# A fused RWKV-5 and dense kernel with a written order: loads from two queues, products in the order of their sums, an arctangent for small h, state products and levels in one run

## The chip, the cores and the metric

The kernel runs on one core of one Trainium2 chip. The metric is the device time of one execution in microseconds. TensorE is called PE here, VectorE DVE, ScalarE ACT, GpSimd POOL and SyncE SP, as in the profile.

## The reference

Two blocks follow each other. The first is a linear attention with decay over 4 batches, 8 heads, 768 steps and a head size of 48; the second is a dense layer of 384 to 2048 to 384 with h - tanh(h) between. Everything is fp32.

```python
for t in range(S):                      # rwkv5, per batch and head
    cur = einsum('bhd,bhe->bhde', u[None] * k[t], v[t])
    y[:, :, t] = einsum('bhd,bhde->bhe', r[t], state + cur)
    state = w[None, :, :, None] * state + einsum('bhd,bhe->bhde', k[t], v[t])
x = y.transpose(0, 2, 1, 3).reshape(B * S, H * D)
h = x @ w_in
out = (h - tanh(h)) @ w_out
```

## The kernel before

**Units.** A unit is 64 steps of two batches (the two halves z of the 128 partitions). There are 24. For a unit the kernel loads r, k and v (L798, two loads each, issued by SP), makes kw = k times a decay (L966), brings r and k into head-by-step form and scales them (rT and kT), and makes three kinds of 64x64 matmuls with `put` (L760): `from_state`, the state products, y from state and rT; `levels`, kT against rT; and `outputs`, y from v and `at`, followed by `to_state`, v against kw. `at` is the masked levels (copy_predicated, L993) with a diagonal from sums of r*k*u (L850, L983, L854 on DVE; L858 on ACT). The result y goes out of the PSUM tile `yk_ps` by ACT copies into `xt` and `rest` (L924), and the state is updated on DVE (L951, L1002). The first two units (`direct`) use k before scaling and load it into `first_k`. Up to unit 12 (`early`), r and k are turned by PE transposes (L810) and the levels go to a bank of their own, `x_ps`; there the state products and the levels stand in one run on PE. From unit 12 on (`two`), r and k are loaded in blocks and turned on DVE (L834, L835), and the levels share `yk_ps` with y. There `from_state` is a step of its own, an ACT copy of two numbers (`between`, L886) follows it, and `levels` waits for that copy. In PSUM, `yk_ps` has two banks; the bank of y is z, and the half of the partitions is i, or i xor z from unit 2 on (`swap`), where i is the head of a pair. So ACT takes y out in three copies, one of both halves and two of one half each, and the rest in three more.

**Tiles.** Two units make a block of 256 steps; there are 12 blocks (j), and of each block 8 tiles (f) of 256 columns of the 2048. For a tile PE makes h (L171, twelve matmuls of 128x256 in the trace's records), in one of two PSUM banks. ACT makes th = tanh(h), tg = tanh(G1 h), s = h^2, q = (s + M1)^2 and a mask `small` where s is below SMALL (L180 to L188). DVE makes g = h - th (L195), then c1 = C4 s tg and c2 = (q + K1) c1 (L197, L199), which is the value of g for small h, where the difference of two close numbers would lose digits, and puts it into g under the mask (L201). Then g goes through w_out: in part of the tiles by plain products o (L209, 128x384), in 71 of them by seven products of half the width (L260, p, 128x192) with three sums of g's quarters made beforehand on POOL (`sums_of_g`, L245 to L249) and mixed columns of w_out. `products` makes them in two parts of four and three, and the first part waits for all three sums. Results are collected on DVE and stored.

**Order.** `Plan` holds all steps as tasks with an engine, a cost and what they wait for. Before, a search at build time (`order`, `follow`) finds an order of all tasks with a model of the engines, and the instructions are recorded in that order; each engine then runs its own in sequence, with semaphores between engines. Matmuls of the identity (`fills`, L688) stand where the model has PE waiting at the start. w_in and w_out come as 64-bit floats and are turned into fp32 on DVE and ACT (L139 to L145) during the first stage.

## Time and profile before

| | |
|---|---|
| Time, median of three runs | 587.51 us (587.33 to 587.73) |
| Span of the profiled execution, first to last instruction | 585.9 us |
| Its own time beside the span | not recorded; the median of the runs is 1.6 us above the span |
| PE busy | 570.1 us, 97% |
| DVE busy | 493.5 us, 84% |
| ACT busy | 395.6 us, 68% |
| POOL busy | 206.1 us, 35% |
| Matmul records on PE | 5493 |
| Mean granted clock of PE | 0.999 |

A row of the timeline has the start and the length in us, the engine, the line, the operation, the tile written and the tile read, the shape and the count; in brackets stands the idle time before it and who ended it. PEld is PE's load of weights, which runs beside its matmuls; SPq and ACTq are the queues on which DMAs are issued. An fp32 matmul has two records. A group of matmuls is reported with the length of its last one's flow through the array, so the time that a group takes is read from its start to the start of the next.

### The profile page before, as it was taken

The numbers are of one execution on the slowest core, as the hardware profiler recorded it, in microseconds if no ns is written. First come the engines' busy times: TensorE is split into PE (matmuls) and PEld (weight loads), VectorE is DVE, ScalarE is ACT, GpSimd is POOL, SyncE is SP. The second block draws the span as 40 slices with busy tenths as digits, with TensorE's granted clock in tenths as the row PEclk, the third lists the DMA queues.
The fourth block names the chain that finished last, engine by engine and source line by source line (L and its number), as shares of the span: only waits on it lengthen the run. The fifth ranks groups of instructions, "written<-read, shape, count | busy, mean of one in ns | idle before, by whom it ended". The sixth has DMA issues, their size and how long they took to land.

```text
span 585.9 us, 14391 instructions
## 1 busy us (share of the span) xinstructions
PE 570.1 (97%) x5493; PEld 481.6 (82%) x5493; DVE 493.5 (84%) x817; ACT 395.6 (68%) x893; POOL 206.1 (35%) x366
## 2 busy tenths in 40 slices
PE   8888999999999999999999999999999999999996
PEld 4566677677777699899889898989999899899995
DVE  5799969999999999977988999888877777646665
ACT  2698889979775585555575785775766765665552
POOL 6002212200000245355455465443534446354420
PEclk9999999999999999999999999999999999999999
DMA  6976986743200121232335432531223300100101
GB/s 123 216 146 123 172 201 122 159 107 80 84 0 1 20 49 28 39 56 45 52 55 90 89 57 41 96 45 32 42 43 48 57 3 8 29 8 1 27 2 31
DMA packets 138549, 38.49 MB, mean 66 GB/s; under 512 B 130760, under 2 KB 132904, under 8 KB 138472
## 3 DMA queue, kind: packets, MB, share of 16 engines
q1 hardware_dynamic: 133308, 30.30, 28.4%
q0 software_dynamic: 4992, 6.99, 5.3%
q8 instruction: 45, 0.74, 0.5%
q14 instruction: 32, 0.26, 0.2%
q10 hardware_dynamic: 172, 0.20, 0.1%
HBM read 31.66 MB, written 4.72 MB: 62 GB/s over the span
## 4 chain that ended last, share of the span: by engine, by line
PE 81%; DVE 9%; ACT 4%; issue 2%; DMA 2%; SPq 1%; POOL 0%; DVEq 0%; ACTq 0%; POOLq 0%
PE h L171 38%; PE p L260 27%; PE o L209 7%; PE yk_ps L760 6%; ACT at L858 1%; SPq L798 1%; DMA xt<-rest 1%; DVE g L201 1%; DVE tg L199 1%; PE h L688 1%; DVE g L195 1%; DVE power L144 1%; DVE at L993 1%; DMA first_k<-in_k_dram 1%; DVE tg L197 1%
## 5 line engine op out<-in xcount | busy, mean ns | idle before, releaser
L171 PE MATMUL h<-xt,w_in_sb 128*128 128x256 f32 x1152 | 281.0, 381 | 1.3 <-DVE w_in_sb L145 0.9
L171 PEld LDWEIGHTS h<-xt,w_in_sb 128*128 128x128 f32 x1152 | 213.1, 190 | 32.6 <-PE x_ps L810 1.1
L245 POOL TENSOR_TENSOR sg<-g 128x256 f32<-128x256 f32 x69 | 54.0, 783 | 224.7 <-DVE g L201 213.9
L260 PE MATMUL p<-mixed,sg 128*128 128x192 f32 x426 | 104.1, 326 | 0.0
L197 DVE SCALAR_TENSOR_TENSOR tg<-s,tg 128x512 f32<-128x512 f32 x96 | 70.2, 731 | 30.5 <-ACT tg L184 21.5
L180 ACT ACTIVATE s<-h 128x512 f32<-128x512 f32 x96 | 57.4, 597 | 54.5 <-PE h L171 54.4
L195 DVE TENSOR_TENSOR g<-h,th 128x512 f32<-128x512 f32 x96 | 65.7, 684 | 29.8 <-ACT tg L184 11.1
L182 ACT ACTIVATE th<-h 128x512 f32<-128x512 f32 x96 | 57.3, 597 | 41.7 <-PE h L171 41.7
L184 ACT ACTIVATE tg<-h 128x512 f32<-128x512 f32 x96 | 57.2, 596 | 37.8 <-PE h L171 36.2
L260 PEld LDWEIGHTS p<-mixed,sg 128*128 128x128 f32 x426 | 75.0, 190 | 0.3 <-issue 0.3
L201 DVE COPY_PREDICATED g<-small,tg 128x512 f32<-128x512 int32 x96 | 71.0, 740 | 4.0
L260 PE MATMUL p<-w_out_sb,g 128*128 128x192 f32 x284 | 71.5, 334 | 0.6 <-DVE parts L222 0.6
L209 PE MATMUL o<-w_out_sb,g 128*128 128x384 f32 x192 | 69.8, 490 | 2.1 <-DVE g L201 2.1
L199 DVE SCALAR_TENSOR_TENSOR tg<-q,tg 128x512 f32<-128x512 f32 x96 | 67.7, 705 | 4.1 <-ACT q L186 1.0
L186 ACT ACTIVATE q<-s,m1b 128x512 f32<-128x512 f32 x96 | 69.8, 727 | 0.5
L188 ACT ACTIVATE small<-s,smallb 128x512 f32<-128x512 f32 x96 | 69.6, 725 | 0.3
L260 PEld LDWEIGHTS p<-w_out_sb,g 128*128 128x128 f32 x284 | 52.1, 190 | 8.6 <-DVE parts L222 1.0
L945 POOL DMA_DIRECT2D xt<-rest x66 | 32.4, 498 | 71.4 <-ACT rest L924 71.1
L209 PEld LDWEIGHTS o<-w_out_sb,g 128*128 128x128 f32 x192 | 35.7, 190 | 19.5 <-issue 1.9
L858 ACT ACTIVATE at<-same,du 128x64 f32<-128x64 f32 x184 | 47.9, 340 | 2.0 <-DVE du L854 1.9
L249 POOL TENSOR_TENSOR sg<-sg,g 128x128 f32<-128x128 f32 x69 | 41.4, 600 | 4.9
L247 POOL TENSOR_TENSOR sg<-sg,g 128x128 f32<-128x128 f32 x69 | 40.2, 582 | 4.9
(129 smaller groups left out, 688.8 us busy)
## 6 DMA issues: line engine op xcount, KB each, us to landing
st<-in_moe_w_out_dram SPq DMA_DIRECT2D x8, 768.0 KB, 4.7
rt<-in_r_dram SPq DMA_DIRECT2D x48, 96.0 KB, 3.0
vt<-in_v_dram SPq DMA_DIRECT2D x48, 96.0 KB, 3.1
st<-in_moe_w_in_dram SPq DMA_DIRECT2D x16, 288.0 KB, 5.7
kt<-in_k_dram SPq DMA_DIRECT2D x44, 96.0 KB, 3.2
out_dram<-o POOLq DMA_DIRECT2D x44, 96.0 KB, 2.2
st<-in_moe_w_in_dram POOLq DMA_DIRECT2D x16, 96.0 KB, 5.6
parts<-in_r_dram SPq DMA_DIRECT2D x48, 32.0 KB, 2.1
```

The costliest lines, as they stand in the source:

```text
L171: self.nc.tensor.matmul(t.h2[:, z], self.w_in_sb[:, t.f // 2, kk, z * 128 : (z + 1) * 128], self.xts[t.j][:, kk].rearrange("p b t -> p (b ...
L180: A.activation(out, t.h, AF.Square)
L182: A.activation(out, t.h, AF.Tanh)
L184: A.activation(out, t.h, AF.Tanh, scale=G1)
L186: A.activation(out, t.s, AF.Square, bias=self.m1b)
L188: A.activation(out, t.s, AF.Relu, bias=self.smallb, scale=-1.0)
L195: V.tensor_tensor(t.g, t.h, t.th, ALU.subtract)
L197: V.scalar_tensor_tensor(t.tg, t.s, C4, t.tg, ALU.mult, ALU.mult)
L199: V.scalar_tensor_tensor(t.tg, t.q, K1, t.tg, ALU.add, ALU.mult)
L201: V.copy_predicated(t.g, t.small.bitcast(I32), t.tg)
L209: self.nc.tensor.matmul(self.outs[i], t.g2[:, z, i * C : (i + 1) * C], self.w_out_sb[:, t.f + z, :], start=t.first and z == 0, stop=t.last ...
L260: self.nc.tensor.matmul(ps[bank][:, half * n : (half + 1) * n], a, b, start=t.first and half == 0, stop=t.last, skip_group_check=True)
```

## The change

1. The search is gone. `ORDER`, a written string of pairs of digits, names the tasks one after the other, and `written` records them in that order.
2. Of the first two units' six pairs of loads the second of each pair is issued by ACT, the first by SP.
3. For tiles that are neither the first nor the last of their block, the seven products stand in another order: first the three that need g alone and the one that needs the first sum's first half, then the three that need the other sums. The first part waits for the first sum alone, the second for the third.
4. s becomes arctan(G2 h), squared in place with a scale (`sq`), and m = s tg takes the place of c1 and c2. `small` is made from the square, with a smaller bound. ACT keeps five steps a tile, DVE has three instead of four.
5. `between` is gone, and `levels` makes the state products itself in all units. y's bank is now i (from unit 2 on), the partition half still i xor z, and the state's halves are turned to fit (z xor i). ACT takes y and the rest out in four copies each.
6. In the first two units `to_state` waits for ACT's copy into xt.

The diff, cut to its core:

```diff
+G1, G2, G3 = 1.00527092, 0.30777497, 1.87096009
+SMALL = 0.05252
+ORDER = (
+    "0F2m2i2j2k2f2g2h00012l2n0J0K0G0H0IbWbW2q323133bX022o033534362t040A3738390C060U050B0T2s070V2rbWbWbWbW082u09bX2v2p"
...
     def act(self, t, x):
+        if x == "sq":
+            A.activation(t.s, t.s, AF.Square, scale=G3)
+            return
...
-            A.activation(out, t.h, AF.Square)
+            A.activation(out, t.h, AF.Arctan, scale=G2)
...
-        elif x == "q":
-            A.activation(out, t.s, AF.Square, bias=self.m1b)
...
-        elif x == "c1":
-            V.scalar_tensor_tensor(t.tg, t.s, C4, t.tg, ALU.mult, ALU.mult)
-        elif x == "c2":
-            V.scalar_tensor_tensor(t.tg, t.q, K1, t.tg, ALU.add, ALU.mult)
+        elif x == "m":
+            V.tensor_tensor(t.tg, t.s, t.tg, ALU.mult)
...
+        of = [(0, 0, g[:, 0], b11), (0, 1, s[:, 2], mixed[:, 1]), (1, 0, g[:, 3], mixed[:, 3]), (1, 1, s[:, 0], mixed[:, 2]),
+              (2, 0, g[:, 2], b21), (2, 1, s[:, 1], mixed[:, 0]), (3, 0, s[:, 3], b22)]
+        if not (t.first or t.last):
+            of = [of[x] for x in (0, 2, 4, 3, 5, 1, 6)]
+        for bank, half, a, b in of[4:] if part else of[:4]:
...
+    def written(self):
+        idle, done = [run for _, _, runs in self.fills for _, run in runs], set()
+        for n in (DIGITS.index(x) * len(DIGITS) + DIGITS.index(y) for x, y in zip(ORDER[::2], ORDER[1::2])):
+            if n < len(self.tasks):
+                t = self.tasks[n]
+                assert all(x.n in done for x in t.after)
+                done.add(n)
+                yield t.run
+            else:
+                yield (idle + [None])[n - len(self.tasks)]
...
-                of = [add("SP", .65, lambda z=z: run(z), after, data=.71) for z in range(2)]
+                of = [add(e, .65, lambda z=z, e=e: run(z, e), after, data=.71) for z, e in enumerate(("SP", "ACT" if n < L else "SP"))]
...
-                            put(y_ps[to(i, z), z, p], state[HEAD[i], z, p], t.rT[HEAD[i], p, z],
+                            put(y_ps[to(i, z), i, p], state[HEAD[i], z ^ i, p], t.rT[HEAD[i], p, z],
...
-            def between():
-
-                A.copy(seen, y_ps[:1, :, 0, 0])
-
             def levels():
-                if not two:
-                    from_state()
+                from_state()
...
-                            put(y_ps[to(i, z), z, p], vt[HALF[z], 2 * p + i], t.at[HALF[z], i, p],
+                            put(y_ps[to(i, z), i if swap else z, p], vt[HALF[z], 2 * p + i], t.at[HALF[z], i, p],
...
-                            put(kv_ps[i * PAD : (i + 1) * PAD, z, p], kw[HALF[z], 2 * p + i], vt[HALF[z], 2 * p + i, :D],
+                            put(kv_ps[i * PAD : (i + 1) * PAD, z ^ i, p], kw[HALF[z], 2 * p + i], vt[HALF[z], 2 * p + i, :D],
...
-                copy(out[:, 0], y[:, 0])
-                for i in range(2):
-                    copy(out[i * PAD : (i + 1) * PAD, 1], y[to(i, 1), 1])
+                for z in range(2):
+                    for i in range(2):
+                        copy(out[i * PAD : (i + 1) * PAD, z], y[to(i, z), i])
...
-            begun = []
-            if two:
-                now = add("PE", .68, from_state, both + [x.rT, b1.xt, b1.rest, b1.add, b2.decay, x.kT], steps=64)
-                begun = [add("ACT", .15, between, [now])]
...
             if direct:
-                now = x.out = add("PE", .6, to_state, [now, x.kw], steps=64)
+                x.out = add("PE", .6, to_state, [now, x.kw, x.xt], steps=64)
...
-                now = add("PE", 1.32, lambda: dense.products(t, 0), [x.sg, mixed[f // 4], b1.o, done.cp, done.diag, done.lev] + b1.empty + b1.emptied[:2], due + 2 * pace, steps=16)
-                x.o = add("PE", .99, lambda: dense.products(t, 1), [now] + b1.emptied, due + 2 * pace + 1.3, steps=12)
+                now = add("PE", 1.32, lambda: dense.products(t, 0), [x.cp, x.sgs[1 if not (t.first or t.last) else 2], mixed[f // 4], b1.o, done.cp, done.diag, done.lev] + b1.empty + b1.emptied[:2], due + 2 * pace, steps=16)
+                x.o = add("PE", .99, lambda: dense.products(t, 1), [now, x.sgs[3]] + b1.emptied, due + 2 * pace + 1.3, steps=12)
```

The order shows three of the places. On PE, around the state products of the first late unit, before (lines 171 and 260 are h and p, 760 the small matmuls; a row of h with x3 is a half):

```order
L171 MATMUL h<-xt,w_in_sb 128x256 x3
L760 MATMUL yk_ps<-rT,state_129 64x64 x16
L171 MATMUL h<-xt,w_in_sb 128x256 x3
L760 MATMUL yk_ps<-rT,kT 64x64 x16
L260 MATMUL p_2476<-w_out_sb,g 128x192
L260 MATMUL p_2476<-mixed,sg 128x192
L260 MATMUL p_2477<-w_out_sb,sg 128x192
```

The same place on PE now (lines 217, 307 and 606 are the same three):

```order
L307 MATMUL p_2485<-mixed,sg 128x192
L307 MATMUL p_2483<-mixed,sg 128x192
L307 MATMUL p_2486<-w_out_sb,sg 128x192
L606 MATMUL yk_ps<-rT,state_126 64x64 x16
L606 MATMUL yk_ps<-rT,kT 64x64 x16
L217 MATMUL h<-xt,w_in_sb 128x256 x6
```

The state products and the levels stand side by side, and the products on either side of them are in their new order. On DVE, from the first unit's kT on, before (kw, rk and du are of units, `at` the masked levels, lines 139 and 140 the first steps of a conversion):

```order
L819 TENSOR_TENSOR kT<-x_ps_149,inverse 128x512
L814 TENSOR_TENSOR rT<-x_ps_149,power 128x512
L993 COPY_PREDICATED at_135<-before,x_ps_149 128x512
L966 TENSOR_TENSOR kw_115<-first_k_125,w_down 128x8x48
L980 COPY_PREDICATED at_135<-same,x_ps_149 128x512
L721 TENSOR_SCALAR flag<-h 1x1
L850 TENSOR_TENSOR rk<-rt_110,first_k_126 128x384
L966 TENSOR_TENSOR kw_116<-first_k_126,w_down 128x8x48
```

On DVE at the same place now:

```order
L665 TENSOR_TENSOR kT<-x_ps_146,inverse 128x512
L660 TENSOR_TENSOR rT<-x_ps_146,power 128x512
L807 TENSOR_TENSOR kw_112<-first_k_122,w_down 128x8x48
L185 TENSOR_SCALAR power<-st 128x768
L186 TENSOR_SCALAR w_in_sb<-st 128x768
L830 COPY_PREDICATED at_132<-before,x_ps_146 128x512
L807 TENSOR_TENSOR kw_113<-first_k_123,w_down 128x8x48
L696 TENSOR_TENSOR rk<-rt_107,first_k_123 128x384
L821 COPY_PREDICATED at_132<-same,x_ps_146 128x512
L189 SCALAR_TENSOR_TENSOR w_in_sb<-w_in_sb,st 128x768
```

The first conversion and the second unit's kw and rk now stand ahead of the first unit's masked levels or between its two steps. On ACT, the first rows of the program now (before, the first was the load of u into `rows` and the second the table load):

```order
L644 DMA vt_116<-in_v_dram 64x8x48
L644 DMA first_k_122<-in_k_dram 64x8x48
L644 DMA rt_106<-in_r_dram 64x8x48
L547 DMA rows<-in_u_dram 4x2x48
L572 ACT_TABLE_LOAD
L572 ACTIVATE warm<-one 128x1
```

Three loads of the first unit stand ahead of u's row. This table load is the only one on the path that runs.

293 lines of the change are left out of this document (74 added, 219 removed).

## The prediction

> **What bounds the kernel now.** I read the page's busy shares first (PE 97%, DVE 84%, ACT 68%), then busy time by stretch, which says where such a mean comes from. Columns: the stretch, its length, then busy us (and instructions) of PE, PEld, DVE, ACT and POOL, the clock, the DMA share and GB/s.
>
> ```profile
> 0.00:45.00 45.00, 37.66 (x619) 24.82 (x619) 33.51 (x64) 27.82 (x76) 9.17 (x37) 1.00 0.84 161
> 45.00:120.00 75.00, 72.19 (x1252) 53.32 (x1253) 69.68 (x120) 66.69 (x178) 19.17 (x38) 1.00 0.77 150
> 120.00:280.00 160.00, 159.31 (x731) 132.29 (x730) 149.12 (x241) 107.96 (x198) 43.30 (x67) 1.00 0.22 47
> 280.00:573.00 293.00, 293.00 (x2858) 264.98 (x2857) 234.29 (x380) 190.04 (x436) 134.49 (x224) 1.00 0.24 41
> ```
>
> From 45 us on PE is the bound: it idles 2.8 us up to 120, 0.7 up to 280, and not at all up to 573. Work taken from another engine buys nothing there; only cheaper PE work does. In the first 45 us PE idles 7.3 us, and part of its busy time is matmuls of the identity that only fill waits (L688). After 573 comes the tail. So there are three places to look: the start, the PE work of the late units, and the tail.
>
> **The late run.** The order on PE around one late unit, 16 matmuls of 64x64 being 32 records in the trace:
>
> ```profile
> 283.86 1.46 PE L171 MATMUL h<-xt,w_in_sb 128*128 128x256 f32 x6
> 285.25 0.69 PE L760 MATMUL yk_ps<-rT,state 48*64 48x64 f32 x32
> 285.87 1.56 PE L171 MATMUL h<-xt,w_in_sb 128*128 128x256 f32 x6
> 287.36 0.69 PE L760 MATMUL yk_ps<-rT,kT 48*64 48x64 f32 x32
> 287.99 0.59 PE L260 MATMUL p<-w_out_sb,g 128*128 128x192 f32 x2
> 288.42 0.49 PE L260 MATMUL p<-mixed,sg 128*128 128x192 f32 x2
> 288.74 0.49 PE L260 MATMUL p<-w_out_sb,sg 128*128 128x192 f32 x2
> 292.31 0.81 PE L171 MATMUL h<-xt,w_in_sb 128*128 128x256 f32 x3
> 293.05 0.69 PE L760 MATMUL yk_ps<-at,vt 64*64 64x64 f32 x32
> 293.56 0.63 PE L760 MATMUL yk_ps<-vt,kw 64*64 64x48 f32 x32
> 294.13 0.59 PE L260 MATMUL p<-w_out_sb,g 128*128 128x192 f32 x2
> 294.56 0.49 PE L260 MATMUL p<-mixed,sg 128*128 128x192 f32 x2
> ```
>
> Two p records take 288.74 - 288.42 = 0.32 us, so one takes 0.16; six h records take 1.29 (0.215 each, as the undisturbed groups of h repeat). From 283.86 to 288.42 lie twelve h (2.58), two p (0.32) and two single runs: 4.56 - 2.90 = 1.66, or 0.83 per run. From 292.31 to 294.56 lie three h (0.65), two p (0.32) and two runs joined: 2.25 - 0.97 = 1.28. Joining saves 1.66 - 1.28 = 0.38 us, which is what entering and leaving the small tiles once costs. The change joins state products and levels in all 12 late units: 12 x 0.38 = 4.6; I take 4.3 (0.36 each), since some neighbours differ, with 3.3 and 4.7 as ends. PE never idles there, so all of it reaches the end. Joined, the state products must wait for kT too, but the planner's row has long had that wait (line 989).
>
> The row halves of the array now meet other PSUM banks: in the outputs both halves write the same bank one behind the other, where they wrote two. Rows: the state products of before write one bank from both halves, the levels two banks, and both run from first record to next group in 0.62 us (285.25 to 285.87, 287.36 to 287.99). So I cost it at nothing. The Trainium skill (TensorEngine Tiling (Array Packing), Gotcha 1: PSUM Pressure) says that different row tiles cannot access the same bank at once; by that rule the outputs would be slower and these two rows would differ. They do not, so the rule does not enter the sum; it stands below as a rival with a small chance.
>
> **The start.** The chain of waits, start and length in us, and the rows that frame the first dense tile:
>
> ```profile
> 8.25 0.63 SPq L798
> 8.93 3.87 DMA first_k<-in_k_dram
> 1.20 1.28 ACTq L701 DMA_DIRECT2D rows<-in_u_dram  x1
> 5.24 0.27 PE L703 MATMUL yk_ps<-ident,rows 8*128 8x8 f32 x1
> 5.74 0.42 DVE L706 TENSOR_SCALAR by<-yk_ps 128x256 f32<-128x256 f32 x1 [3.59 <-ACT saved L717]
> 20.91 1.55 PE L688 MATMUL h<-ident 128*128 128x512 f32 x3 [1.41 <-issue]
> 45.20 0.72 DVE L201 COPY_PREDICATED g<-small,tg 128x512 f32<-128x512 int32 x1
> 46.07 1.53 PE L209 MATMUL o<-w_out_sb,g 128*128 128x384 f32 x4 [1.56 <-DVE g L201]
> ```
>
> PE reaches full use with the first o at 46.07, which waits for g of tile 0, the last of a DVE chain from 5.74 to 45.92:
>
> ```profile
> 5.74:45.92 40.18, 33.55 (x57) 1.00 0.91 174
> DVE at L993 <- ACT at L858: 2.2, 1, 2.2
> DVE w_in_sb L143 <- ACT st L142: 1.6, 2, 1.3
> DVE at L993 <- PE x_ps L760: 1.4, 1, 1.4
> ```
>
> So 33.5 us of work and 6.6 us of waits. What a step takes when the next stands right behind it, from the chain of waits:
>
> ```profile
> 48.02 0.47 DVE state L1002
> 55.57 0.87 DVE w_out_sb L143
> 59.86 0.60 DVE tg L197
> ```
>
> Three terms move this chain:
> - Work ahead of it. Counted in the order, 56 DVE instructions stood from the decay to this g; now 51. Gone from ahead of it are one conversion of 768, three products of 384 and, with c1 and c2 made one m, one of 512. That is 0.87 + 3 x 0.47 + 0.60 = 2.9 us earlier.
> - The decay starts later. u's row stood first on ACT's queue (issued 1.20 to 2.48); now three loads of the first unit stand ahead of it, and w's row is fourth on SP. At the 0.63 of SP's row that is 1.9 us; some of it may be free, since the row at 5.24 stands behind fills on PE. I take 1.5 later, between 0.5 and 2.2.
> - Waits. The order now puts conversions and the next unit's products where DVE stood waiting for the levels, the diagonals and st, 5.2 of the 6.6 us. I take half, 2.5, between 0 and 5.
>
> Together 2.9 - 1.5 + 2.5 = 3.9; I take 4.0 earlier, between 0 and 7 (all of PE's 7.3 us idle). PE has the same useful work ahead of its first o in both orders, and as many fills of each width, so nothing there grows. The stall at 20.91, where PE waited 1.41 us for nothing that the profile shows, may come again; it is in the lower end, as is a new wait: in the first two units the products for the state wait for ACT's copy of xt, with the next unit's transposes queued behind them on PE.
>
> The loads themselves: twelve go out on SP at 0.63 each, 7.6 us; with half of them on ACT the last goes out up to 3.8 us sooner. The row 8.93 shows what is behind them: a load that was issued in 0.63 took 3.87 to land, and the DMA share was 0.91 over this stretch. So I give the two queues nothing of their own. The Trainium skill (DMA: Bandwidth & Descriptors, Issuing engines are not separate DMA queues) says the same against this part of the change: issuing from two engines saves only the time of issuing. Taken in full those 3.8 us would put the time at 575.0; the row speaks for the rule.
>
> **The activation.**
>
> ```profile
> L197 DVE SCALAR_TENSOR_TENSOR tg<-s,tg 128x512 f32<-128x512 f32 x96 | 70.2, 731 | 30.5 <-ACT tg L184 21.5
> L199 DVE SCALAR_TENSOR_TENSOR tg<-q,tg 128x512 f32<-128x512 f32 x96 | 67.7, 705 | 4.1 <-ACT q L186 1.0
> L195 DVE TENSOR_TENSOR g<-h,th 128x512 f32<-128x512 f32 x96 | 65.7, 684 | 29.8 <-ACT tg L184 11.1
> L186 ACT ACTIVATE q<-s,m1b 128x512 f32<-128x512 f32 x96 | 69.8, 727 | 0.5
> L180 ACT ACTIVATE s<-h 128x512 f32<-128x512 f32 x96 | 57.4, 597 | 54.5 <-PE h L171 54.4
> ```
>
> Two DVE steps (731 + 705 ns) become one of a tensor_tensor's form (684): 96 x 0.75 = 72 us off DVE. ACT's q becomes a square without the bias column, which I put at the 597 ns of the plain square. Neither reaches the end after 45 us, where PE has no wait to lose; it widens the margin. If the cover were gone (PE waiting for g everywhere), this would be the largest term. ACT copies each unit out of yk_ps in eight pieces instead of six; behind the outputs the rows above show p and not the next unit's state products, so nothing there. The products in the order of their sums let four of seven start after one POOL sum; PE did not wait for POOL, so nothing either. That no second table load stands in the new order is read from its rows.
>
> **The tail.** ACT's and DVE's rows ahead of the last o:
>
> ```profile
> 576.55 0.32 ACT L279 COPY e<-p 128x192 f32<-128x192 f32 x1
> 577.42 0.73 DVE L201 COPY_PREDICATED g<-small,tg 128x512 f32<-128x512 int32 x1
> 578.04 0.34 DVE L288 TENSOR_TENSOR e<-e,p 128x192 f32<-128x192 f32 x1
> 578.44 2.85 PE L209 MATMUL p<-w_out_sb,g 128*128 128x384 f32 x8 [0.30 <-DVE e L288]
> ```
>
> e was ready for DVE at 576.87 but stood behind the last g until 578.04. With one step less and more products queued behind the last h, g is done sooner and o follows its products: 0.4 us, between 0 and 1.
>
> **Sum.** 4.3 + 4.0 + 0.4 = 8.7 us. The profiled span is 585.9, the median of the three runs 587.5, 1.6 above it, which I carry over: 585.9 - 8.7 = 577.2 as span, 577.2 + 1.6 = **578.8 us**.
>
> **Rivals.**
> - The start gives nothing (the stall comes back, the late decay row eats the rest): only the joined runs and the tail count, 587.5 - 4.3 = 583.2 to 582.8. For it: the stall at 20.91, and one term of three that runs the other way. Against: 2.9 us are counted instructions. 20%.
> - The start gives all: 7 + 4.7 + 1 = 12.7, so 574.8. 13%.
> - Slower: h has two banks, so an h waits until th, s, tg and g of the second tile before it are done. Counted in the orders at the cadences above, ten h now stand under 4 us of matmuls behind the end of that tile, down to 2.6; before, two did, both in the first stage. Three ACT passes of 0.6 and a g of 0.68 make 2.5 us when both engines are free. If ACT's work for the units stands ahead each time, ten waits of 1 us give 10, and 578.8 + 10 = 588.8. It decides from 8.7 us of waits on. Against: ACT is busy 190 of 293 us there. 4%.
> - Slower too, by the rule on banks: 1.28 - 0.83 = 0.45 us is what 32 more records add to a run; at half the overlap as much again in the outputs of 22 units, 10 us: 588.8. 2%.
> - It does nothing on net, start against gain: within 0.2% (1.2 us, about what a measurement of this kernel can tell) of 587.5. 3%.
>
> My forecast has the other 58%. The range of 574.0 to 583.5 leaves out the slower rivals and the far end of each bound. Faster 0.91, same 0.03, slower 0.06.
>
> **What would show it.** Right: yk_ps from rT and state with levels in one run of 64, 1.28 us more than its neighbours need; the first o of L254 near 42; PE without idle from there to the end. Wrong: a first o at 45 or later (the start's terms), h waiting for ACT or DVE in the late stage (the bank rival), outputs of 64 records taking over 1.5 us (the PSUM rival), or more than one table load.

## The result and the profile after

The changed kernel takes 583.39 us (median of 8 runs, 581.88 to 586.07), the kernel before beside it on the same chip 587.64 us (8 runs, 587.33 to 589.09). The ratio is 0.9934, with a 95% interval of 0.9922 to 0.9946: 4.25 us faster, just under half of the forecast 8.7, and at the upper end of the stated range of 574.0 to 583.5. A later series of the same kernel gave 582.56 us (4 runs, 581.96 to 583.45), a ratio of 0.9900 (0.9876 to 0.9925). The single runs of the new order scatter more than those of the old one, and the two series differ by 0.3% themselves, so a difference of 1 or 2 us between two kernels of the new order is not clear of noise.

Busy time by stretch, changed kernel, same columns and bounds as before the change:

```profile
0.00:45.00 45.00, 38.18 (x612) 24.80 (x612) 31.17 (x59) 25.41 (x70) 9.29 (x38) 0.92 0.86 161
45.00:120.00 75.00, 72.90 (x1265) 54.58 (x1262) 60.24 (x107) 69.96 (x205) 16.27 (x34) 1.00 0.59 118
120.00:280.00 160.00, 159.64 (x807) 132.07 (x809) 135.85 (x218) 109.28 (x196) 44.09 (x71) 1.00 0.30 63
280.00:573.00 293.00, 292.23 (x2813) 267.92 (x2805) 198.54 (x330) 198.53 (x456) 133.70 (x224) 1.00 0.24 41
```

DVE's load fell everywhere (234 to 199 us in the last row), and PE is nearly as full behind 45 us as it was (it now idles 2.1, 0.4 and 0.8 us in the last three rows). What is new stands in the first row: the granted clock was 1.00 over the first 45 us and is 0.92.

PE around one late unit of the changed kernel, state products and levels now in one run of 64 records:

```profile
292.57 0.49 PE L307 MATMUL p<-w_out_sb,sg 128*128 128x192 f32 x2
292.99 0.69 PE L606 MATMUL yk_ps<-rT,state 48*64 48x64 f32 x32
293.50 0.65 PE L606 MATMUL yk_ps<-rT,kT 48*64 48x64 f32 x32
294.08 0.59 PE L307 MATMUL p<-w_out_sb,g 128*128 128x192 f32 x2
294.51 0.49 PE L307 MATMUL p<-mixed,g 128*128 128x192 f32 x2
```

From 292.57 to 294.51 lie four p records (0.65) and the joined run: 1.94 - 0.65 = 1.29, where two single runs cost 1.66 by the prediction's rows.

The outputs of such a unit, whose two row halves now write one bank:

```profile
302.29 0.49 PE L307 MATMUL p<-w_out_sb,sg 128*128 128x192 f32 x2
302.71 0.69 PE L606 MATMUL yk_ps<-at,vt 64*64 64x64 f32 x32
303.23 0.63 PE L606 MATMUL yk_ps<-vt,kw 64*64 64x48 f32 x32
303.79 0.59 PE L307 MATMUL p<-w_out_sb,g 128*128 128x192 f32 x2
304.22 0.49 PE L307 MATMUL p<-mixed,sg 128*128 128x192 f32 x2
```

From 302.29 to 304.22 lie again four p records and one joined run: 1.93 - 0.65 = 1.28, the same as the outputs cost before.

The start of the changed kernel, engines mixed, in order of time:

```profile
2.24 0.72 ACTq L644 DMA_DIRECT2D rt<-in_r_dram  x1
4.26 1.97 SPq L171 DMA_DIRECT2D st<-in_moe_w_in_dram  x2
4.98 1.23 ACTq L547 DMA_DIRECT2D rows<-in_u_dram  x1
9.57 0.24 PE L549 MATMUL yk_ps<-ident,rows 8*128 8x8 f32 x1 [2.48 <-issue]
10.65 5.99 PE L534 MATMUL h<-ident 128*128 128x512 f32 x8
16.47 0.60 PE L529 MATMUL h<-ident,twice 128*128 128x128 f32 x4
17.62 0.56 DVE L807 TENSOR_TENSOR kw<-first_k,w_down 128x384 f32<-128x384 f32 x1 [3.40 <-ACT w_down L562]
25.90 0.33 PE L606 MATMUL x_ps<-rT,kT 48*64 48x64 f32 x4 [1.67 <-issue]
46.30 2.17 PE L254 MATMUL o<-w_out_sb,g 128*128 128x384 f32 x6 [0.24 <-DVE w_out_sb L191]
```

u's row goes out at 4.98 (before: 1.20), so PE transposes the rows at 9.57 (before: 5.24). Eight fill records then take 5.99 us, 0.75 each (in the kernel before, four at 15.84 took 1.56 us, 0.39 each), and `twice`, the transposes that give `w_down`, stands behind them. The first o comes at 46.30; it was forecast near 42 and stood at 46.07.

The first o cuts the kernel in two. Behind it lie 581.5 - 46.30 = 535.2 us (span 581.5), before 585.9 - 46.07 = 539.8: 4.6 us gained there, against 4.7 forecast for the joined runs and the tail. In that part PE's busy time fell from 532.5 to 527.9 us and its idle time stayed (7.4 and 7.3 us); the last o (L254, L209 before) starts 528.2 us behind the first instead of 532.4, and from there to the end it takes 7.0 us instead of 7.5. Ahead of the first o nothing was gained, against 4.0.

DVE from the start of the decay to the first o (stretch, length, busy us and instructions, clock, DMA share, GB/s), first the kernel before, then the changed one:

```profile
5.74:46.07 40.33, 33.70 (x57) 1.00 0.91 173
```

```profile
9.85:46.30 36.45, 31.62 (x53) 0.92 0.85 155
```

So the first o comes at the decay's start plus DVE's work plus its waits: 5.74 + 33.70 + 6.63 = 46.07 before, 9.85 + 31.62 + 4.83 = 46.30 now. Work and waits shrank by 2.1 and 1.8, and the decay's start took back 4.1.

### The profile page after: what moved, and what is told of

It reads as the page before. It is cut to its first block, busy times and chain, and to the rows that moved or that the text cites. A ratio compares the mean times of both kernels' runs of the same rounds, so it can differ in the third digit from the quotient of the medians.

```text
span 581.5 us, 14198 instructions
## 1 busy us (share of the span) xinstructions
PE 567.1 (98%) x5493; PEld 482.1 (83%) x5493; DVE 429.1 (74%) x720; ACT 403.5 (69%) x925; POOL 203.3 (35%) x366
## 3 DMA queue, kind: packets, MB, share of 16 engines
q1 hardware_dynamic: 130140, 29.71, 27.9%
## 4 chain that ended last, share of the span: by engine, by line
PE 88%; DVE 4%; DMA 3%; ACT 2%; issue 2%; SPq 1%; POOL 1%; ACTq 0%; DVEq 0%
PE h L217 42%; PE p L307 27%; PE o L254 10%; PE yk_ps L606 6%; PE h L534 1%; PE x_ps L656 1%; SPq L644 1%; DMA vt<-in_v_dram 1%; DMA xt<-rest 1%; DMA first_k<-in_k_dram 1%; PE x_ps L606 1%; PE p L254 0%; ACT xt L765 0%; ACT rest L765 0%; DVE at L830 0%
## 5 line engine op out<-in xcount | busy, mean ns | idle before, releaser
L217 PE MATMUL h<-xt,w_in_sb 128*128 128x256 f32 x1152 | 266.4, 381 | 1.5 <-DMA xt<-rest 0.7
L290 POOL TENSOR_TENSOR sg<-g 128x256 f32<-128x256 f32 x69 | 56.8, 824 | 169.8 <-DVE g L246 137.4
L307 PE MATMUL p<-mixed,sg 128*128 128x192 f32 x426 | 92.1, 326 | 0.0
L244 DVE TENSOR_TENSOR tg<-s,tg 128x512 f32<-128x512 f32 x96 | 69.1, 721 | 25.2 <-ACT s L224 17.7
L246 DVE COPY_PREDICATED g<-small,tg 128x512 f32<-128x512 int32 x96 | 73.0, 765 | 15.8 <-ACT small L235 12.9
L231 ACT ACTIVATE th<-h 128x512 f32<-128x512 f32 x96 | 56.5, 593 | 32.5 <-PE h L217 31.9
L254 PE MATMUL o<-w_out_sb,g 128*128 128x384 f32 x192 | 66.5, 489 | 0.5 <-DVE g L246 0.3
L224 ACT ACTIVATE s<-s 128x512 f32<-128x512 f32 x96 | 60.3, 632 | 1.2
L254 PEld LDWEIGHTS o<-w_out_sb,g 128*128 128x128 f32 x192 | 35.6, 190 | 21.2 <-ACT parts L278 0.7
L292 POOL TENSOR_TENSOR sg<-sg,g 128x128 f32<-128x128 f32 x69 | 39.4, 575 | 3.3
L294 POOL TENSOR_TENSOR sg<-sg,g 128x128 f32<-128x128 f32 x69 | 38.4, 561 | 3.9
L345 POOL DMA_DIRECT2D out_dram<-o x44 | 23.9, 545 | 39.8 <-DVE o L339 23.0
```

Source lines behind the costliest of these rows:

```text
L217: self.nc.tensor.matmul(t.h2[:, z], self.w_in_sb[:, t.f // 2, kk, z * 128 : (z + 1) * 128], self.xts[t.j][:, kk].rearrange("p b t -> p (b ...
L224: A.activation(t.s, t.s, AF.Square, scale=G3)
L231: A.activation(out, t.h, AF.Tanh)
L244: V.tensor_tensor(t.tg, t.s, t.tg, ALU.mult)
L246: V.copy_predicated(t.g, t.small.bitcast(I32), t.tg)
L254: self.nc.tensor.matmul(self.outs[i], t.g2[:, z, i * C : (i + 1) * C], self.w_out_sb[:, t.f + z, :], start=t.first and z == 0, stop=t.last ...
```

## The experiments

The first theory was that the late rows, and the cold fills behind them, ate the start's gain; the rival, that the start is bound elsewhere and only the work behind the first o counts. All kernels are the changed one with the edit shown, but for the last. Unless said otherwise an edit moves entries of the written order, shown as the engine's rows. Each first o below is read from the one profiled run of its kernel, and that run need not be a typical one: with the rows first, with only their issues first, and with the rows first on one queue it took 585.33, 586.76 and 585.32 us, 0.9 to 2.7 above the kernel's median, in the others at most 1.1 above, but for the new activation in the kernel before (2.1).

**The rows first again.**

```diff
 (ACT, SP) +L547 DMA rows ahead of every load, as before the change
 (PE)
 L534 MATMUL h<-ident 128x512 x2
+L549 MATMUL yk_ps<-ident,rows 128x8
 L656 MATMUL x_ps_146<-ident,first_k_122 128x128 x4
 L534 MATMUL h<-ident 128x256
-L549 MATMUL yk_ps<-ident,rows 128x8
```

> The changed kernel with one thing put back: u's row is first on ACT's queue and w's row first on SP's again, and PE transposes both right behind its first fills, as before the change. Nothing else moves. Theory A (the start's gain was lost because the decay began 4.1 us later): rows near 5.3 in place of 9.57, the twice transposes near 11.5 in place of 16.47, the first o of L254 at 41.5 to 43 in place of 46.30, and a time 3 to 5 us under the changed kernel's 583.4, so 578.5 to 580.5. Rival B (the start is set by the landing of the loads, by DVE's work or by the stall of PE with no releaser, and the late rows were hidden): first o within 1 us of 46.3 and a time of 582.5 to 584. A time between the two says that part of the 4.1 us only moves into DVE's waits.

Measured: 584.47 us, ratio 0.9936 (0.9918 to 0.9954), no gain. Its start, engines mixed:

```profile
5.23 0.27 PE L549 MATMUL yk_ps<-ident,rows 8*128 8x8 f32 x1
8.17 1.09 PE L656 MATMUL x_ps<-ident,first_k 128*128 128x128 f32 x4 [2.67 <-DMA first_k<-in_k_dram]
11.67 4.69 PE L534 MATMUL h<-ident 128*128 128x512 f32 x8
16.20 0.60 PE L529 MATMUL h<-ident,twice 128*128 128x128 f32 x4
17.35 0.56 DVE L807 TENSOR_TENSOR kw<-first_k,w_down 128x384 f32<-128x384 f32 x1 [4.14 <-ACT w_down L562]
26.48 0.33 PE L606 MATMUL x_ps<-rT,kT 48*64 48x64 f32 x4 [2.52 <-issue]
48.59 2.82 PE L254 MATMUL o<-w_out_sb,g 128*128 128x384 f32 x8 [0.24 <-DVE w_out_sb L191]
```

```profile
5.54:48.59 43.05, 31.63 (x53) 0.96 0.91 162
```

The decay begins 4.3 us earlier, and DVE's waits grow from 4.8 to 43.05 - 31.63 = 11.4: k now lands later, `twice` stays at 16.2. The late rows had been hidden behind that. The time lies just above the rival's band and far from the theory's, so the theory falls in this form.

**Only the issues first**, the transpose left where it was:

```diff
 (ACT, SP) +L547 DMA rows ahead of every load; PE unchanged
```

> Only the two issues of the rows are put first on their queues; the transpose of the rows stays on PE behind the transpose of k and a fill. The rows are then there near 5, but PE reaches their transpose behind k, which lands near 6.7 now: 7.3 to 7.6. Theory A (the start follows the decay): about half to two thirds of the gain of the run with both, first o near 43.5 to 44.5, time 580.5 to 582. Rival B (the rows were hidden): 582.5 to 584, as in the other run.

Measured: 584.05 us, ratio 0.9921 (0.9895 to 0.9947), first o at 49.30. That is nearer the rival's answer, but four runs from 581.46 to 586.76 decide little alone.

**Three of the four wide fills ahead of the rows.**

```diff
 (PE)
+L534 MATMUL h<-ident 128x512 x3
 L549 MATMUL yk_ps<-ident,rows 128x8
 L656 MATMUL x_ps_146<-ident,rt_106 128x128 x4
-L534 MATMUL h<-ident 128x512 x4
+L534 MATMUL h<-ident 128x512
```

> The changed kernel with three of the four wide fills that stand on PE ahead of the twice transposes moved ahead of the transpose of the rows, where PE idled 2.48 us; the rows still come late. Theory A2 (the fills cost the start a second time: with the clock down behind the idle time they ran until 16.6, and twice, ready at 13.47, stood behind them for 3 us): twice near 13.6 to 14, first o 1.5 to 2.7 us earlier (43.6 to 44.8), time 580.8 to 582. Rival B2 (DVE has enough other work there, or waits for the loads anyway): first o near 46 and 583 to 584.

Measured: 583.92 us, ratio 0.9931 (0.9916 to 0.9947), the rival's time; first o at 47.22. PE's rows:

```profile
12.02 0.23 PE L549 MATMUL yk_ps<-ident,rows 8*128 8x8 f32 x1
15.97 0.66 PE L529 MATMUL h<-ident,twice 128*128 128x128 f32 x4 [2.27 <-ACT twice L560]
```

The fills ran mostly at half rate there (PE loaded their weights 0.85 us apart, at 8.69, 9.54 and 10.39) and pushed the rows from 9.57 to 12.02, so `twice` gained 0.5 us and the first o none. The edit did not give its theory a fair trial.

**The rows first, every load on SP's queue.**

```diff
-                of = [... for z, e in enumerate(("SP", "ACT" if n < L else "SP"))]
+                of = [... for z, e in enumerate(("SP", "SP"))]
```

> As the run with the rows first and transposed first, but every load of the first unit goes out on SP's queue, none on ACT's. It tells what the two queues are worth by themselves. The prediction gave them nothing. On that: the same time as with two queues, within 0.6 us. Rival (the issues count): k's and r's second halves are issued 1.5 to 3 us later, their transposes come 1 to 2 us later, and the time is 1 to 2 us above that of the run with two queues.

Measured: 583.75 us, ratio 0.9924 (0.9906 to 0.9943), beside 584.47 with two queues: the same within the intervals.

**All of it at once**: the rows, then k and r, then ub and v; one fill in the idle time ahead of k, one in place of four ahead of `twice`.

```diff
 (PE)
 L534 MATMUL h<-ident 128x512 x2
+L549 MATMUL yk_ps<-ident,rows 128x8
+L534 MATMUL h<-ident 128x512
 L656 MATMUL x_ps_146<-ident,first_k_122 128x128 x4
 L534 MATMUL h<-ident 128x256
-L549 MATMUL yk_ps<-ident,rows 128x8
 L656 MATMUL x_ps_146<-ident,rt_106 128x128 x4
-L534 MATMUL h<-ident 128x512 x4
+L534 MATMUL h<-ident 128x512
```

> The first four runs left the time at 583.75 to 584.47: moving the rows or the fills alone gives nothing, so the first theory has fallen in that form. In all of them PE idled 2.3 to 2.7 us somewhere before 16, its granted clock was at half for a stretch ahead of 31, and twice was transposed at 15.3 to 18. This kernel takes all of it away at once: the rows first, then k and r (ub and v behind them), one wide fill in the idle time ahead of k, and one in place of four ahead of twice. Theory C (PE's clock: idle time ahead of 16 puts PE at half rate, and the fills then stand in front of twice): PE has no idle over 1 us ahead of 12, full clock from about 7.4 on as before the change, twice at 9.5 to 10.5, first o at 41 to 43.5, time 578 to 581. Rival D (from twice on the start is bound by the landing of the conversions' loads, by DVE, or by PE's stall behind its 219th matmul): twice at 10 too, but first o not ahead of 45, and 582.5 to 584.

Measured: 581.72 us, ratio 0.9906 (0.9888 to 0.9925); first o at 43.31, in the upper part of theory C's band, the time between the two bands and not clear of the changed kernel's 582.56 to 583.39. `twice` came at 11.77 and not at 10. ACT's rows say why:

```profile
9.85 0.17 ACT L563 COPY saved<-yk_ps 128x8 f32<-128x8 f32 x1 [3.75 <-DMA rt<-in_r_dram]
11.09 0.62 ACT L560 COPY twice<-inverse 128x512 f32<-128x512 f32 x1 [1.08 <-DVE kT L665]
```

`saved` could be copied from 5.5 on (the rows' transpose ended at 5.50) and DVE had `inverse` at 8.52; both copies stood on ACT behind issues of the second unit's loads, which waited.

**The same with one queue.**

```diff
-                of = [... for z, e in enumerate(("SP", "ACT" if n < L else "SP"))]
+                of = [... for z, e in enumerate(("SP", "SP"))]
```

> The kernel without idle time, with every load of the first unit on SP's queue. If two queues are worth nothing: within 0.7 us of that kernel. If ACT's issues stand in the way of its copies (saved came at 8.42 and twice's copy at 9.37 behind three issues, against 6.00 and 8.55 with one queue): up to 1 us faster. If the loads' landing counts: k and r come 1 to 1.5 us later and the time is 1 to 2 us longer.

Measured: 582.29 us, ratio 0.9905 (0.9890 to 0.9919), first o at 44.70. `twice` came at 8.97, but a new wait stands behind it, POOL's and ACT's rows:

```profile
12.00 0.26 POOL L739 COPY extra<-vt 128x96 f32<-128x96 f32 x1 [5.40 <-DMA vt<-in_v_dram]
13.71 1.28 ACT L709 ACTIVATE kU<-kT,w_u 128x128 f32<-128x128 f32 x4 [4.79 <-POOL w_u L564]
```

**That copy of v behind w_u on POOL**, one queue:

```diff
 (POOL)
-L739 COPY extra_130<-vt_116 128x6x16
 L521 TENSOR_SCALAR ok<-saved 128x4
...
 L564 TENSOR_TENSOR w_u<-saved 128x4
 L171 DMA st<-in_moe_w_in_dram 16x3x256 x2
+L739 COPY extra_130<-vt_116 128x6x16
```

> The kernel without idle time and with one queue, in which PE did idle after all, 4.10 us from 10.06 on: kU waited for w_u on POOL, and w_u stood behind a copy of v's columns that waited for v's load (12.00). Here that copy stands behind w_u on POOL; nothing else moves. Theory C (PE's idle time and its clock at the start): no idle over 1.5 us ahead of 20, twice near 9, the first unit's outputs near 15 to 17 in place of 21.94, first o at 40.5 to 42.5 in place of 44.70, time 578.5 to 580.5. Rival D (behind twice the conversions' loads bind): first o not ahead of 43.5, time 581 to 582.5.

Measured: 582.45 us, ratio 0.9905 (0.9890 to 0.9919), first o at 44.73: no gain, rival D's answer. kU now came 4.6 us earlier, and PE waited for the next thing, the second unit's r (11.99 before the change):

```profile
16.87 1.09 PE L656 MATMUL x_ps<-ident,rt 128*128 128x128 f32 x4 [5.17 <-DMA rt<-in_r_dram]
```

**The same with two queues for the first unit only.**

```diff
-                of = [... for z, e in enumerate(("SP", "ACT" if n < L else "SP"))]
+                of = [... for z, e in enumerate(("SP", "ACT" if n < 1 else "SP"))]
```

> The same with the first unit's loads from two queues and the second unit's all on SP, so that ACT's copies stand behind no load of the second unit. In the two kernels before, k and r of the first unit were transposed at 6.15 and 7.10 with one queue and at 7.30 and 9.22 with two: the loads share the DMA engines, and the later ones take from the first. If that is so, two queues are 0 to 1.5 us slower here than one; if the second unit's loads on ACT were the cause, the two kernels are alike within 0.5 us or two queues are faster by up to 1 us.

Measured: 580.40 us, ratio 0.9880 (0.9865 to 0.9894), the fastest here, 1.2% under the kernel before; its four runs (579.98 to 581.82) lie below all twelve of the changed kernel. First o at 42.70:

```profile
5.55:42.70 37.15, 31.92 (x53) 0.95 0.91 184
```

Waits 5.2, decay at 5.55: the prediction's start (4.0 us earlier) is nearly there, 3.4. It came with two queues and not with one: 2.05 us faster, more than either expectation allowed. In PE's rows the first unit's k and r were transposed later with two queues (6.74 and 9.56) than with one (6.09 and 7.00), as was expected; the second unit's r came earlier (15.39 and 16.87). SP's rows fit that: with half of the first unit's loads on ACT, SP came to that r at 6.05 and not at 8.00. Whether this is what gave the 2 us was not tested.

**The weights' loads behind the second unit's**, alone. The new order issues them at 4.26 on SP and 5.35 on POOL; before the change it was 10.96 and 9.22.

```diff
 (SP)
 L644 DMA vt_116<-in_v_dram 64x8x48
-L171 DMA st<-in_moe_w_in_dram 48x3x256 x2
 L644 DMA rt_107<-in_r_dram 64x8x48
 L644 DMA first_k_123<-in_k_dram 64x8x48
 L644 DMA vt_117<-in_v_dram 64x8x48
+L171 DMA st<-in_moe_w_in_dram 48x3x256 x2
 (POOL) the other two st likewise
```

> The changed kernel with one thing moved: the first loads of the dense weights (st, two on SP and two on POOL, 4.26 and 5.35 in the changed kernel; 10.96 and 9.22 in the one before) stand behind the second unit's loads again, as before the change. The rows still come late. Theory F (the weights' loads take the DMA engines from the units' loads): r and k of the second unit land earlier, but PE reaches them only behind the late twice (16.47), so the gain by itself is small: first o 45 to 46.5, 582.5 to 583.5. If the conversions of the weights set DVE's chain instead, they begin some 5 us later and the time is 1 to 3 us longer: 584.5 to 586.5.

Measured: 583.13 us, ratio 0.9922 (0.9895 to 0.9950), first o at 45.92, beside 582.56 for the changed kernel in the same series. No gain alone, as expected.

**The same with the other hindrances gone**, one queue and two (the edits of the two kernels above put together):

```diff
 (SP)   -L171 DMA st x2 ahead of, +L171 DMA st x2 behind the second unit's r, k, v
 (POOL) -L171 DMA st x2 ahead of, +L171 DMA st x2 behind L564 TENSOR_TENSOR w_u<-saved
```

> The kernel with one queue, with the copy of v's columns behind w_u, and now with the weights' loads behind the second unit's. In it PE waited 5.17 us for the second unit's r (16.87; 11.99 before the change). Theory F: that r is transposed at 12 to 13.5, the first unit's outputs come at 15 to 17.5 in place of 21.97, first o at 41 to 43 in place of 44.73, time 578.5 to 581. Rival G (the bytes have to come in any order, and DVE then waits for the weights in place of PE for the units): DVE waits 3 us or more for st behind 12, first o at 44 to 46, time 582 to 584.

> The same with the first unit's loads from two queues, where the second unit's r came at 15.39. Theory F: the weights' loads no longer compete with the first units' from both queues; r of the second unit at 11.5 to 13.5, first o at 40.5 to 42.5 in place of 42.70, time 578 to 580.5. Rival G: as with one queue, no gain on 580.4, or 1 to 2 us longer.

Measured: 585.42 us, ratio 0.9965 (0.9947 to 0.9982), and 585.19 us, 0.9950 (0.9930 to 0.9970): slower than the changed kernel and than the same two kernels with the weights early (582.45 and 580.40), first o at 47.87 and 47.92. That is rival G's way, but later than its bands (first o 44 to 46, 582 to 584). With one queue the second unit's r came at 12.32, as theory F had it, and then, DVE's and PE's rows:

```profile
18.91 0.56 DVE L185 TENSOR_SCALAR power<-st 128x768 uint32<-128x768 uint32 x1 [7.45 <-DMA st<-in_moe_w_in_dram]
22.17 0.92 PE L606 MATMUL yk_ps<-at,vt 64*64 64x64 f32 x24 [3.41 <-DVE at L821]
```

The bytes have to come in some order. With the weights first PE waits for the units, with the units first DVE waits for the weights. In the new order the weights' early place is no loss: moved back it gave nothing alone and cost 3 to 5 us here.

**The changed kernel once more**, beside these three, with no edit:

> The changed kernel once more, on the same chip as the other three, so that they stand beside it: 582 to 586, as in its first runs.

Measured: 582.56 us, first o at 46.43.

The starts side by side: where the decay begins on DVE, DVE's work and waits from there to the first o, and what lies behind it, each from its own profiled run.

| kernel | decay | work | waits | first o | behind it |
|---|---|---|---|---|---|
| before | 5.74 | 33.7 | 6.6 | 46.07 | 539.8 |
| changed | 9.85 | 31.6 | 4.8 | 46.30 | 535.2 |
| changed, later series | 9.69 | 31.6 | 5.1 | 46.43 | 535.1 |
| rows first | 5.54 | 31.6 | 11.4 | 48.59 | 534.9 |
| rows issued first only | 9.95 | 31.6 | 7.7 | 49.30 | 535.6 |
| fills ahead | 12.29 | 31.8 | 3.1 | 47.22 | 535.2 |
| rows first, one queue | 5.54 | 31.6 | 10.4 | 47.59 | 535.9 |
| no idle time | 5.54 | 31.9 | 5.9 | 43.31 | 536.2 |
| no idle time, one queue | 5.29 | 32.0 | 7.4 | 44.70 | 536.3 |
| copy of v behind, one queue | 5.24 | 31.9 | 7.6 | 44.73 | 536.3 |
| copy of v behind, two queues | 5.55 | 31.9 | 5.2 | 42.70 | 535.4 |
| weights behind | 8.36 | 31.7 | 5.9 | 45.92 | 535.9 |
| weights behind, all, one queue | 5.35 | 31.7 | 10.8 | 47.87 | 535.0 |
| weights behind, all, two queues | 5.35 | 31.7 | 10.9 | 47.92 | 535.9 |

In all kernels of the new order the last column is 534.9 to 536.3 and the work column 31.6 to 32.0. Nearly all that differs is the sum of the decay's start and the waits. An earlier decay mostly comes with longer waits, so no single step gained its own size.

**The joined runs apart again** in nine of the twelve late units (in three the order leaves no such place):

```diff
+            x.lev.begin = from_state if two else None
...
+                at = max(y for y in range(i) if y in tasks and tasks[y].engine == "PE")
...
+            if i in begins:
+                yield begins[i]
```

> The changed kernel with the state products of nine of the twelve late units issued one matmul group earlier, so that they form a run of 32 of their own again (in three units the order leaves no such place). Theory: each joined run saved 0.36 us, so the time from the first o to the end grows by 9 x 0.36 = 3.2 us, from 535.2 to 538.4, and the time to 586 to 587. Rival (the gain of the change is from elsewhere, and the runs cost the same): 583 to 584.

Measured: 586.07 us, ratio 0.9974 (0.9961 to 0.9988), 2.7 us above the changed kernel; 537.6 us behind the first o, 2.4 more. PE around the same unit:

```profile
291.41 0.49 PE L307 MATMUL p<-mixed,sg 128*128 128x192 f32 x2
291.83 0.69 PE L615 MATMUL yk_ps<-rT,state 48*64 48x64 f32 x32
292.45 0.92 PE L307 MATMUL p<-mixed,sg 128*128 128x192 f32 x4
293.21 0.49 PE L307 MATMUL p<-w_out_sb,sg 128*128 128x192 f32 x2
293.63 0.69 PE L615 MATMUL yk_ps<-rT,kT 48*64 48x64 f32 x32
294.25 0.59 PE L307 MATMUL p<-w_out_sb,g 128*128 128x192 f32 x2
294.68 0.49 PE L307 MATMUL p<-mixed,g 128*128 128x192 f32 x2
```

From 291.41 to 294.68 lie ten p records (1.63) and the two runs: 3.27 - 1.63 = 1.64, against 1.29 joined. The theory holds; the last 0.8 us of 3.2 are within the scatter of 1.4 us in the last column above.

**The old activation in the new order.**

```diff
-            A.activation(out, t.h, AF.Arctan, scale=G2)
+            A.activation(out, t.h, AF.Square)
...
-            A.activation(t.s, t.s, AF.Square, scale=G3)
+            t.q = self.tmp("q")
+            A.activation(t.q, t.s, AF.Square, bias=self.m1b)
...
-            V.tensor_tensor(t.tg, t.s, t.tg, ALU.mult)
+            V.scalar_tensor_tensor(t.tg, t.s, C4, t.tg, ALU.mult, ALU.mult)
+            V.scalar_tensor_tensor(t.tg, t.q, K1, t.tg, ALU.add, ALU.mult)
...
```

> The changed kernel's order with the activation of before: two steps of DVE in place of one in each of 96 tiles (some 70 us more work on DVE), the square with a bias column. If DVE was no bound behind the first o, as predicted: first o 0.6 to 1.5 us later for the steps ahead of it, nothing or little behind it, so 583.5 to 585.5. Rival (the lighter activation is what made the kernel faster, and DVE is late for PE in this order): 586 or more, with PE idle behind g in the stretch from 45 to 120.

Measured: 612.93 us, ratio 1.0428 (1.0405 to 1.0452): the rival's answer, and far above its 586. First o at 49.00; behind it 563.1 us, 27.9 more than in the changed kernel. PE alone by stretch, and one row of its waits (us in all, times, longest):

```profile
120.00:280.00 160.00, 151.19 (x663) 1.00 0.28 59
280.00:573.00 293.00, 285.01 (x2802) 0.99 0.25 42
```

```profile
PE h L219 <- DVE g L245: 6.6, 8, 1.7
```

PE idles 8.8 and 8.0 us where it idled 0.4 and 0.8, and from 45 to 120, where the rival looked for it, 3.4 where it idled 2.1. Behind the first o its idle time grew from 7.3 to 25.6 us and its busy time, at a clock of 0.98 to 0.99 in the late stretches, from 527.9 to 537.5. Eight times an h waits for the g of an earlier tile, the prediction's first slower rival; in the changed kernel such a wait stands once, 0.5 us. So this order, as written, needs the lighter activation.

**The new activation in the kernel before**, planned anew by its planner:

```diff
 (before.py)
-            A.activation(out, t.h, AF.Square)
+            A.activation(out, t.h, AF.Arctan, scale=G2)
...
-            A.activation(out, t.s, AF.Square, bias=self.m1b)
+            A.activation(t.s, t.s, AF.Square, scale=G3)
...
-            V.scalar_tensor_tensor(t.tg, t.s, C4, t.tg, ALU.mult, ALU.mult)
-            V.scalar_tensor_tensor(t.tg, t.q, K1, t.tg, ALU.add, ALU.mult)
+            V.tensor_tensor(t.tg, t.s, t.tg, ALU.mult)
...
```

> The kernel before with the new activation alone, its order planned anew by the planner of before with one DVE step less in each of 96 tiles. As predicted (from 45 us on PE was the bound, so DVE's relief buys nothing by itself there): 539 to 540.5 us from the first o to the end, a first o 0 to 3 us earlier, time 584.5 to 588. Rival (the relief lets PE run without waits that the trace doesn't name): under 584.

Measured: 593.89 us, ratio 1.0108 (1.0083 to 1.0132): slower than both expectations. First o at 50.64, 543.5 us behind it. PE's longest wait there is 3.3 us, ended by nothing that the profile shows.

No gain from the relief alone. But the planner made another order with more waits, so the run does not give the relief's own worth; only that it does not come by itself.

## Why the prediction was half right

**The joined runs and the tail were right.** Forecast 4.3 + 0.4 = 4.7, measured 4.6 behind the first o: 4.2 up to the last o and 0.4 behind it. Joined, a pair costs 1.29 instead of 1.64, twelve pairs 4.2 us, and undoing nine pairs cost 2.4 us behind the first o (2.7 in the time). That the sum came out to a tenth is partly luck, since the same part scatters by 1.4 us from kernel to kernel. PE stayed nearly without idle, as said (0.8 of 293 us in the late stretch). The time came to lie inside the stated range although the start gave nothing; for the start that is luck.

**The start's 4.0 failed**, and first its step "The decay starts later": "I take 1.5 later, between 0.5 and 2.2". It was 4.1. That step counted three loads ahead of u's row at SP's 0.63, 1.9 us. In the rows above the issue moved from 1.20 to 4.98, 3.8 us, twice that: the last of three loads on ACT went out at 2.24 to 2.96, and then ACT waited 2.0 us more before u's row. And the transpose then stood on PE behind k and a fill. The other two terms had the right sign and were a little large. The work ahead of g fell by 2.9 as counted (32.83 to 29.90 us, 56 to 51 instructions), but one conversion of w_out_sb only moved from ahead of g to between g and the first o, which now waits for it and no longer for g (the 0.24 wait at 46.30); up to the first o the work fell by 2.1. The waits fell by 1.8 and not 2.5.

**A term at nothing failed with it**: "as many fills of each width, so nothing there grows". The count was right (22 records of 512 and 14 of 256 ahead of the first o in both kernels). But eight of the wide ones now stood ahead of `twice`, in part at half rate, for 5.99 us, and `twice` came at 16.47 instead of 9.52. What that cost by itself no run shows; with the rows first and most of these fills gone `twice` came at 11.77.

**The deeper error was to add the three as if they were independent.** With the rows put back, the decay began 4.3 us earlier and the waits grew by 6.6. The start is held from several sides at once: the landing of k and r, fills at half rate ahead of `twice`, ACT's copies behind issues that wait, w_u behind a copy of v, the second unit's r, the weights: each was the next wait in one of the runs. The weights' loads, 6.7 us earlier on SP and ahead of the second unit's, stood in the order and were not in the working at all; moving them back gained nothing. The rows first and fewer fills together brought the first o 2.8 us ahead of the kernel before (43.31), with the copy of v behind w_u and the second unit's loads off ACT's queue 3.4 of the 4.0, and only then was the time clear of the changed kernel's. The rival "the start gives nothing" was the case: worked out at 582.8 to 583.2, measured 583.39. Its reason, the late decay row and the stall, is not shown: with the rows back nothing was gained, and what the stall costs was not tested alone.

**The two queues at nothing** held in three pairs of four, two queues named first (584.47 and 583.75, 581.72 and 582.29, 585.19 and 585.42); in one they were 2.05 us faster (580.40 and 582.45). In the first two of the three both units had two queues, in the last and in the fourth pair the first unit alone. The Trainium skill (DMA: Bandwidth & Descriptors, Issuing engines are not separate DMA queues) says that issuing from two engines saves only issuing time; the three pairs agree, and the fourth stays open.

**The activation at nothing** was right for what the change gained: nothing behind the first o is left over for it. The DVE step cost 721 ns and the square on ACT 632, where 684 and 597 were taken:

```profile
L244 DVE TENSOR_TENSOR tg<-s,tg 128x512 f32<-128x512 f32 x96 | 69.1, 721 | 25.2 <-ACT s L224 17.7
L224 ACT ACTIVATE s<-s 128x512 f32<-128x512 f32 x96 | 60.3, 632 | 1.2
```

But "it widens the margin" undersold it: the new order has spent that margin, and without it takes 29 us more. A term of zero in the difference was not a term of zero in the kernel.

**The rivals that fell.** Both row halves writing one bank cost nothing: the outputs take 1.28 us with one bank and took 1.28 with two, where the rival had 0.45 more. In the changed kernel h waits for ACT or DVE for 0.7 us in all. What stays open: why single runs of the new order scatter over 4 us (of the first eight the fastest had a mean granted clock of 1.000 and the three slowest 0.990 to 0.993, but one at 583.33 had 0.991); how near to the bytes' own limit the best start (42.70) is; and what the products' new order and the four ACT copies are worth, which no run changed alone. An order planned with the landing times measured here was not tried.

## What to carry to other kernels

Before a start-up term is booked, write the chain as one sum (start, work, waits of the engine that ends last) and ask of each wait what would stand behind it once it is gone: in these starts, with the DMA engines 0.75 to 0.95 busy, a saved microsecond mostly turned into the next wait. Count every instruction that a new order moves on a queue, and say what waits for it; here the weights' loads had moved by 6.7 us and were not counted, though putting them back proved no gain. Name the instruction that the end of the chain waits for after the change too: here it was no longer g. In a stretch where PE hardly idles, a cheaper run of matmuls arrives at the end, and its gain was forecast from two pairs of rows to within the scatter of the runs.

## What the runs showed of the hardware

**PE stopped at one place of its program, in step with an instruction packet.** In ten of the seventeen profiled runs PE stopped behind its 219th or 220th matmul record for 1.4 to 3.3 us with no releaser (1.41 before, 1.67 changed, 2.52 with the rows first). In the kernel with the rows first one instruction packet of 0.02 MB was moved between 23.7 and 25.0, and PE, which had stopped at 23.96, went on at 26.48:

```profile
q8 instruction: 1, 0.02, 5.5%
```

In all ten runs PE went on 1.4 to 1.7 us after such a packet had ended. In the seven others the packet had ended at least 1.6 us before PE came to that place; in the fastest kernel it was there by 19.6, and PE came after 22. That PE waited for this packet, its own code, is read from these times; the profile does not name whose code it is. Most slices of the DMA view read 9, full, in both stretches. The Trainium skill (Runtime: NRT & Kernel Launch, Instruction fetch mechanics) says that the cost of crossing from one 16 KB block to the next is mostly hidden; if these packets are such blocks, in ten of the seventeen starts it was not.

**The granted clock fell behind short idle times.** Changed kernel, PE alone (stretch, length, busy us and records, clock, DMA share, GB/s):

```profile
6.00:9.00 3.00, 1.06 (x6) 0.94 0.99 226
9.00:12.00 3.00, 2.43 (x7) 0.50 1.33 183
12.00:15.00 3.00, 3.00 (x5) 0.50 1.29 189
```

PE idled 0.73 us ahead of 6.03 and 2.48 us ahead of 9.57. The clock was still 1.00 from 8.20 to 8.60 and 0.53 from 8.60 to 9.00, so it fell when PE had idled 1.5 us since the end of its last fill at 7.10; it then stayed at half until past 15. The Trainium skill (TensorE: Matmul & The Clock Gate, Part 1: The HAM clock gate) puts the fall behind an idle window of about 3.4 us; here 1.5 us of full idleness with a little work ahead of it was enough. The length of one idle time does not decide it alone: in the fastest kernel PE idled 1.79 us ahead of 9.56, and the transposes of r behind it still took 0.66 us at a clock of 1.00.

The column can also hide a half rate at the very start. With the rows first PE's transposes of k at 8.17 took 1.09 us, as long as r's did at a clock of 0.50 in the changed kernel (1.11 at 9.74), where k's took 0.63; the column reads 1.00 from 6 to 15 there. So the rate of the first microseconds is better read from the rows.
